# Loading the value windows of the first batch ahead of the weight stages, and weight stages through GpSimd's queue

## The chip, the cores and the metric

The kernel runs on one core of a Trainium2 chip. The metric is the time of one execution on the device in microseconds (us). A profile records one execution: its span runs from the first to the last instruction of the core.

## The reference

Four batches, eight heads, 576 positions, 64 values per head. Three stages follow one another:

```
# attention, per head, two parts that are added
out_d     = softmax(scale * mean4(q) @ mean4(k).T) @ mean4(v)       # 144 x 144, on means of 4 positions
out_local = softmax over |i - j| < 4 of (scale * q @ k.T)  @ v      # a band of 7 keys
x = repeat4(out_d) + out_local                                      # laid out as (batch, 576, 512)

# first gated layer
h = relu(x @ w_in)                        # 512 -> 1024
x = (h * sigmoid(conv3(h))) @ w_out       # 1024 -> 512

# second gated layer
out = (sigmoid(conv5(x)) * (x @ w_val)) @ w_out2
```

`w_in`, `w_out`, `w_val`, `w_out2` and the two convolutions' weights come as 64-bit floats; the kernel turns them into 32-bit floats itself, and splits each into a high and a low part for three matmuls in the place of one.

## The kernel before

**Work.** Attention goes by head pairs, four a batch, sixteen steps `s` in all. A step `s` has eight slots (`att_slots`, which stands in the big function): scores of the band (`loc_s`), scores of the means (`down_s`), then in slots 2 and 3 the values of the *step before* (`loc_av`, two halves) between the normalisations (`loc_n`, `down_n`), in slots 4 and 5 the transposes of the next head pair's k and q (`prep_k`, `prep_q`), and in slots 6 and 7 the rest. `prep_q` also averages v over four positions (`pool_v`: two adds on VectorE, tiles `ldv` and `vd`). The results of `loc_av` are tile `xo`.

**Two forms of v.** `pool_v` reads v in tile `ldv`. `loc_av` reads v by key blocks of 32 positions, in tile `ldw`: for each of 24 blocks of queries the 32 keys around it. For the first batch, `load_v_first` (L270) brings `ldv` in two halves (head pairs 0 and 1, then 2 and 3), and `load_vw_first` (L283) brings `ldw` for all eight heads in 24 loads of 64 KB. For later batches `load_v` (L239) and `load_vw` (L302) do it step by step.

**Weights.** `Weights` keeps a list of 16 jobs: eight pieces of `w_in`, then eight of `w_out`, each 128x512 (512 KB of 64-bit numbers). `load` issues the transfer of the next piece into one of three `stage` buffers (two for the last ones); `split` turns a landed piece into 32 bits (one step on ScalarE, tile `stage`, then four on VectorE) and into its parts (one on ScalarE, one on VectorE, tiles `win` and `wout`). Three loads stand ahead of the steps; each later load follows a split, and its transfer waits until the last reader of its buffer is done: eight at places listed in `EARLY`, the others between matmul units of the first batch.

**Order.** Every transfer is issued on SyncE's queue (SP). SP issues in order. The program gives SP's loads eight completion counters in turn, so that a load also waits until the load eight places before it has landed. The order on the other engines is set when the program is built, by a scheduler that estimates when each operand will be there; `ordered` pins it for the steps of the first batch (PE, VectorE, ScalarE), `beneath` lets the splits fill in between. ScalarE (ACT), VectorE (DVE) and SP run what they have strictly in that order. Nearly all instructions of DVE and ACT have line L151 and those of PE L141, which are the helpers that record them, so tiles are named instead.

Of the kernel before, what the change touches and what calls it, by code (L numbers as in the profile page):

```python
# [10 lines left out]
I32 = mybir.dt.int32  # L11
# [52 lines left out]
def kernel(  # L64
# [13 lines left out]
    nc = tc.nc  # L78
# [5 lines left out]
    HP = H // 2  # L84
# [15 lines left out]
    PW = 512  # L100
# [33 lines left out]
    def key_start(j):  # L134

        return min(max(QB * j - 4, 0), S - KB)
# [54 lines left out]
    class Weights:  # L191
# [10 lines left out]
            self.staged = []  # L202
            self.n = 0

        def load(self):
            if not self.jobs:
                return
            dst, src, j, f0 = self.jobs.pop(0)
            rows = src[j * 128 : j * 128 + 128]
            t, w = self.stage(self.n)  # L210
            self.n += 1
            if src.dtype == F32:
                nc.sync.dma_start(out=w, in_=rows[:, f0 : f0 + PW])
            else:
                nc.sync.dma_start(out=t, in_=rows.bitcast(I32)[:, 2 * f0 : 2 * (f0 + PW)])
            self.staged.append((t, w, src.dtype == F32, dst, j, f0))

        def split(self):
# [18 lines left out]
    def load_v(b, hp):  # L237
        t = ap.tile([HD, 2, 2, 4, D], F32, tag="ldv", name="ldv", bufs=1)
        nc.sync.dma_start(  # L239
            out=t.rearrange("p e s r d -> p e s (r d)"),  # L240
            in_=v[b, 2 * hp : 2 * hp + 2].rearrange("h (s p r) d -> p h s (r d)", s=2, r=4),
        )
        T["ldv", b, hp] = t
# [20 lines left out]
    def load_v_first(part):  # L264

        if part == 0:
            first["v"] = keep.tile([HD, H, 2, 4, D], F32, tag="wout1", name="ldv")
        n = H // 2
        t = first["v"][:, part * n : part * n + n]
        nc.sync.dma_start(  # L270
            out=t.rearrange("p h s r d -> p (h s) (r d)"),
            in_=v[0, part * n : part * n + n].rearrange("h (s p r) d -> p (h s) (r d)", s=2, r=4),
        )
        for hp in range(part * HP // 2, (part + 1) * HP // 2):
            T["ldv", 0, hp] = first["v"][:, 2 * hp : 2 * hp + 2]

    def load_vw_first():

        vw = keep.tile([128, NG, H, D], F32, tag="wout0", name="ldw")
        for g in range(NG):  # L280
            for c in range(4):
                k0 = key_start(c * NG + g)
                nc.sync.dma_start(  # L283
                    out=vw[KB * c : KB * c + KB, g], in_=v[0, :, k0 : k0 + KB].rearrange("h k d -> k h d")
                )
        for hp in range(HP):
            T["ldw", 0, hp] = vw[:, :, 2 * hp : 2 * hp + 2]
# [241 lines left out]
    def prep_k(s):  # L529
        transp(T.pop(("ldk", *where(s))), "k", scale)  # L530
        if HP <= s + 1 < NSTEP:
            load(k, "ldk", *where(s + 1))

    def prep_q(s):
        transp(T.pop(("ldq", *where(s))), "q", 1.0)
        pool_v(*where(s))
        if HP <= s + 1 < NSTEP:
            load(q, "ldq", *where(s + 1))
            load_v(*where(s + 1))
# [212 lines left out]
            unit(fn)  # L752

    make_identity(nc, ident)
    for hp in range(HP):
        load(k, "ldk", 0, hp)
        load(q, "ldq", 0, hp)
        if hp % 2 == 0:
            load_v_first(hp // 2)
    for h in HT:  # L760
        nc.gpsimd.memset(h, 0.0)
    nc.gpsimd.memset(mask, 0.0)
# [4 lines left out]
    for c, g, n, off in spans + [(0, 0, 1, 0), (3, NG - 1, 1, QB * (NB - 1) - key_start(NB - 1))]:  # L767
        m = m3[32 * c : 32 * c + 32, g : g + n]
        for sgn in (1, -1):
            nc.gpsimd.affine_select(  # L770
                out=m,
                in_=m,
# [11 lines left out]

    W = Weights([(win, w_in), (wout, w_out)], stage)

    nw = 3 * KF + 5 * KM
    cw = mp.tile([nw, 384], I32, tag="cv", name="cw", bufs=3)
    cwf = cw[:, 256:].bitcast(F32)
    for src, o, m in ((conv3, 0, 3 * KF), (conv5, 3 * KF, 5 * KM)):  # L790
        if src.dtype == F32:
            nc.sync.dma_start(out=cwf[o : o + m], in_=src.rearrange("t (f p) -> (t f) p", p=128))
        else:
            nc.sync.dma_start(
                out=cw[o : o + m, :256], in_=src.bitcast(I32).rearrange("t (f p) -> (t f) p", p=256)
# [6 lines left out]
        mm(p[:, :nw], cwf, ident[:nw, :nw], is_transpose=True)  # L802
        vec.tensor_copy(cwt, p[:, :nw])

    for _ in range(3):
        W.load()
    load_vw_first()
    load_v(1, 0)
    load(k, "ldk", 1, 0)
    load(q, "ldq", 1, 0)  # L810
# [122 lines left out]
```

## Time and profile before

| | |
|---|---|
| median of 3 runs | 521.6 us (517.53 to 523.5) |
| the profiled execution | 523.79 us |
| its span | 521.7 us |
| PE busy | 453.0 us (87%) |
| DVE busy | 358.2 us (69%) |
| ACT busy | 266.0 us (51%) |
| POOL (GpSimd) busy | 6.1 us (1%), 25 instructions |
| moved by DMA | 39.58 MB, mean 76 GB/s |
| mean granted TensorE clock | 0.905 |

PE's share is high over the span as a whole, but not in its first third: the page's slices of 13 us show PE at 4 to 7 tenths up to about 120 us, and at 9 for most of the time behind it. The row "PEclk" of the same slices gives the granted clock, which is at half (1.2 GHz of 2.4) from 26 us to some 90 us.

### The profile page before, as it was taken

How to read it: one execution, taken by the hardware profiler on the slowest of the kernel's cores; microseconds unless marked ns; L12 is line 12 of the kernel's file. 1: busy time of each engine (PE TensorE's matmuls, PEld its weight loads, DVE VectorE, ACT ScalarE, POOL GpSimd, SP SyncE). 2: the span in 40 equal slices, each digit the busy share in tenths (PEclk: the TensorE clock that was granted, in tenths of full speed). 3: DMA queues.
4: the chain of work that ended last, by engine and by line, in shares of the span. 5: the costliest groups of instructions: out<-in, count | busy, mean ns of one | idle time of the engine just before them, and what ended most of it. 6: DMA issues, size and time to landing. Idle time of an engine off the chain costs nothing.

```text
span 521.7 us, 13808 instructions
## 1 busy us (share of the span) xinstructions
PE 453.0 (87%) x5961; PEld 412.7 (79%) x5961; DVE 358.2 (69%) x655; ACT 266.0 (51%) x564; POOL 6.1 (1%) x25
## 2 busy tenths in 40 slices
PE   5747565468977999899899999999968999999997
PEld 4546544357976999899899889999958999889885
DVE  3517678789997344897866799503989999964130
ACT  1504535467784443877545678414877365542122
POOL 4000000000000000000000000000000000000000
PEclk9955556598998999999799999999987999999999
DMA  8957124343441214224133121003112000120102
GB/s 204 222 130 164 52 82 114 113 132 111 119 113 29 67 43 93 48 58 98 28 74 79 37 64 32 14 21 122 40 41 81 10 33 2 60 102 20 62 21 102
DMA packets 70963, 39.58 MB, mean 76 GB/s; under 512 B 59050, under 2 KB 65526, under 8 KB 70902
## 3 DMA queue, kind: packets, MB, share of 16 engines
q1 hardware_dynamic: 70902, 38.70, 28.0%
q8 instruction: 47, 0.77, 0.6%
q14 instruction: 14, 0.11, 0.1%
HBM read 33.96 MB, written 4.72 MB: 74 GB/s over the span
## 4 chain that ended last, share of the span: by engine, by line
PE 59%; DVE 21%; DMA 9%; ACT 7%; SPq 2%; issue 1%; ACTq 0%; DVEq 0%
PE pb L141 19%; PE pa L141 12%; PE pc L141 10%; PE pd L141 10%; DVE cv L151 5%; DVE stage L151 4%; PE avl L141 3%; DMA ldv<-in_v_dram 3%; DMA stage<-in_moe_w_in_dram 2%; ACT ed L151 2%; DMA ldq<-in_q_dram 2%; DVE hglo L151 2%; SPq L283 1%; PE tp L141 1%; DMA stage<-in_moe_w_out_dram 1%
## 5 line engine op out<-in xcount | busy, mean ns | idle before, releaser
L141 PE MATMUL pb<-hghi,wout 128*128 128x288 f32 x512 | 105.5, 314 | 4.7 <-ACT hghi L151 4.7
L141 PE MATMUL pa<-xhi,win 128*128 128x288 f32 x512 | 103.0, 308 | 3.6 <-DVE xo L151 3.6
L141 PEld LDWEIGHTS pb<-hghi,wout 128*128 128x128 f32 x512 | 80.6, 197 | 8.6 <-ACT hghi L151 5.6
L141 PEld LDWEIGHTS pa<-xhi,win 128*128 128x128 f32 x512 | 78.1, 192 | 6.9 <-DVE xo L151 3.9
L141 PE MATMUL pb<-hglo,wout 128*128 128x288 f32 x256 | 57.5, 307 | 2.0 <-DVE hglo L151 2.0
L151 DVE SCALAR_TENSOR_TENSOR cv<-h,cwt,cv 128x576 f32<-128x576 f32 x64 | 51.9, 811 | 7.5 <-ACT cv L151 7.1
L141 PE MATMUL pa<-xlo,win 128*128 128x288 f32 x256 | 55.5, 299 | 0.0
L141 PE MATMUL pc<-ys,wval 128*128 128x288 f32 x384 | 51.3, 294 | 0.0
L141 PEld LDWEIGHTS pc<-ys,wval 128*128 128x128 f32 x384 | 51.1, 188 | 0.3
L151 DVE SCALAR_TENSOR_TENSOR g<-y,cwt,g 128x576 f32<-128x576 f32 x64 | 49.5, 814 | 0.0
L141 PEld LDWEIGHTS avl<-et,ldw 32*64 32x64 f32 x1536 | 30.1, 150 | 22.3 <-issue 8.5
L141 PE MATMUL avl<-et,ldw 32*64 32x24 f32 x1536 | 34.2, 227 | 15.5 <-DMA ldw<-in_v_dram 9.2
L141 PEld LDWEIGHTS pb<-hglo,wout 128*128 128x128 f32 x256 | 43.0, 197 | 3.5 <-DVE hglo L151 3.4
L141 PE MATMUL pd<-wout,hghi 128*128 128x512 f32 x144 | 44.7, 394 | 0.0
L141 PEld LDWEIGHTS pa<-xlo,win 128*128 128x128 f32 x256 | 42.0, 193 | 0.0
L151 DVE TENSOR_TENSOR xo<-avl,od 128x288 f32<-128x288 f32 x32 | 14.2, 444 | 32.3 <-PE avl L141 32.3
L151 ACT ACTIVATE ed<-ed,smd 72x144 f32<-72x144 f32 x64 | 21.4, 404 | 23.6 <-DVE smd L151 23.6
L141 PEld LDWEIGHTS pd<-wout,hghi 128*128 128x128 f32 x144 | 26.7, 187 | 6.3
L151 ACT ACTIVATE cv<-cv 128x576 f32<-128x576 f32 x32 | 21.9, 683 | 15.3 <-DVE cv L151 14.9
L151 DVE TENSOR_TENSOR hglo<-cv,hghi 128x576 fp32r<-128x576 f32 x32 | 24.1, 753 | 6.8 <-ACT hghi L151 6.8
L151 ACT ACTIVATE hghi<-cv 128x576 fp32r<-128x576 f32 x32 | 21.8, 680 | 13.0 <-DVE cv L151 12.9
L151 ACT ACTIVATE ed<-sd,mxd 72x144 f32<-72x144 f32 x64 | 23.3, 370 | 10.0 <-DVE mxd L151 9.2
(87 smaller groups left out, 695.2 us busy)
## 6 DMA issues: line engine op xcount, KB each, us to landing
stage<-in_moe_w_out_dram SPq DMA_DIRECT2D x12, 512.0 KB
out_dram<-o SPq DMA_DIRECT2D x18, 256.0 KB
stage<-in_moe_w_in_dram SPq DMA_DIRECT2D x8, 512.0 KB
ldv<-in_v_dram SPq DMA_DIRECT2D x13, 288.0 KB
ldk<-in_k_dram SPq DMA_DIRECT2D x26, 144.0 KB
ldq<-in_q_dram SPq DMA_DIRECT2D x26, 144.0 KB
ldw<-in_v_dram SPq DMA_DIRECT2D x48, 48.0 KB
stage<-in_moe_w_val_dram SPq DMA_DIRECT2D x4, 512.0 KB
```

Of the source, the lines that this page charges most:

```text
L141: last["pe"] = nc.tensor.matmul(*a, **kw)
L151: last[self.key] = getattr(self.engine, name)(*a, **kw)
L283: nc.sync.dma_start(out=vw[KB * c : KB * c + KB, g], in_=v[0, :, k0 : k0 + KB].rearrange("h k d -> k h d"))
```

## The change

`Weights.load` gets an argument `queue` that is GpSimd's queue unless another is named; the first three loads name SP. So the five other pieces of `w_in` and the eight of `w_out` are issued by GpSimd (POOL), and only the first three by SP. At the start, only head pairs 0 and 1 of k and q and the first half of v are issued first; then come the 24 loads of `load_vw_first`, then the three weight stages, then k and q of head pairs 2 and 3 with the second half of v between them. Sizes, buffers and arithmetic are the same.

```diff
-        def load(self):
+        def load(self, queue=nc.gpsimd):
...
             if src.dtype == F32:
-                nc.sync.dma_start(out=w, in_=rows[:, f0 : f0 + PW])
+                queue.dma_start(out=w, in_=rows[:, f0 : f0 + PW])
             else:
-                nc.sync.dma_start(out=t, in_=rows.bitcast(I32)[:, 2 * f0 : 2 * (f0 + PW)])
+                queue.dma_start(out=t, in_=rows.bitcast(I32)[:, 2 * f0 : 2 * (f0 + PW)])
...
-    for hp in range(HP):
+    for hp in range(2):
         load(k, "ldk", 0, hp)
         load(q, "ldq", 0, hp)
-        if hp % 2 == 0:
-            load_v_first(hp // 2)
+        if hp == 0:
+            load_v_first(0)
+    load_vw_first()
...
     W = Weights([(win, w_in), (wout, w_out)], stage)
 
+    for _ in range(3):
+        W.load(nc.sync)
+    for hp in range(2, HP):
+        load(k, "ldk", 0, hp)
+        load(q, "ldq", 0, hp)
+        if hp == 2:
+            load_v_first(1)
...
-    for _ in range(3):
-        W.load()
-    load_vw_first()
     load_v(1, 0)
```

On SP, from its start, the program before has this order (72x8x256 is a half of v, 32x8x64 one load of the key blocks):

```order
L252 DMA ldk<-in_k_dram 96x2x384
L252 DMA ldq<-in_q_dram 96x2x384
L270 DMA ldv<-in_v_dram 72x8x256
L252 DMA ldk<-in_k_dram 96x2x384
L252 DMA ldq<-in_q_dram 96x2x384
L252 DMA ldk<-in_k_dram 96x2x384
L252 DMA ldq<-in_q_dram 96x2x384
L270 DMA ldv<-in_v_dram 72x8x256
L252 DMA ldk<-in_k_dram 96x2x384
L252 DMA ldq<-in_q_dram 96x2x384
L794 DMA cw<-in_moe_conv_w_dram 24x256
L794 DMA cw<-in_moe_conv_w_dram 20x256
L215 DMA stage<-in_moe_w_in_dram 128x1024 x3
L283 DMA ldw<-in_v_dram 32x8x64 x24
```

And with the change:

```order
L252 DMA ldk<-in_k_dram 96x2x384
L252 DMA ldq<-in_q_dram 96x2x384
L270 DMA ldv<-in_v_dram 72x8x256
L252 DMA ldk<-in_k_dram 96x2x384
L252 DMA ldq<-in_q_dram 96x2x384
L283 DMA ldw<-in_v_dram 32x8x64 x24
L215 DMA stage<-in_moe_w_in_dram 128x1024 x3
L252 DMA ldk<-in_k_dram 96x2x384
L252 DMA ldq<-in_q_dram 96x2x384
L270 DMA ldv<-in_v_dram 72x8x256
L252 DMA ldk<-in_k_dram 96x2x384
L252 DMA ldq<-in_q_dram 96x2x384
```

The key blocks moved ahead of the weight stages and of five loads that steps 2 and 3 read; the second half of v now stands behind all of these.

On ACT, in the first matmul units of the first batch, the order before and the order now differ from the place where the first piece of `w_out` is converted. One piece of it before (`h`, `cv`: gate of the first layer; `stage`: first conversion step of a weight piece; `od`: result of the means' attention):

```order
L151 ACTIVATE h_78<-pa 128x576
L151 ACTIVATE cv<-h_78,cwt 128x576
L151 ACTIVATE stage<-stage 128x512
L151 ACTIVATE od<-avd 128x144
L151 ACTIVATE wout_1223<-stage 128x512
L151 ACTIVATE cv<-cv 128x576
```

And now:

```order
L151 ACTIVATE h_78<-pa 128x576
L151 ACTIVATE cv<-h_78,cwt 128x576
L151 ACTIVATE od<-avd 128x144
L151 ACTIVATE wout_1223<-stage 128x512
L151 ACTIVATE stage<-stage 128x512
L151 ACTIVATE cv<-cv 128x576
```

The conversion of a piece, which waits for a transfer, stands behind `od` now. DVE's order changes in the same stretch in the same manner, some rows up and some down; PE's order is the same throughout.

## Rows read from the trace of the kernel before

**Rows 1.** Engines by stretch: from:to, length, busy us (instructions), clock, DMA share, GB/s.
```profile
0.00:20.00 20.00, 13.04 (x216) 11.53 (x218) 8.49 (x19) 7.59 (x19) 5.62 (x21) 1.00 0.93 215
20.00:40.00 20.00, 10.72 (x226) 8.57 (x224) 5.36 (x14) 2.36 (x10) 0.00 (x0) 0.67 0.66 156
...
40.00:60.00 20.00, 14.61 (x302) 12.65 (x300) 14.40 (x35) 9.05 (x25) 0.00 (x0) 0.50 0.46 108
140.00:160.00 20.00, 14.76 (x200) 13.42 (x202) 20.00 (x39) 15.59 (x33) 0.11 (x1) 0.99 0.30 77
...
180.00:200.00 20.00, 20.00 (x333) 18.68 (x332) 8.14 (x18) 7.82 (x21) 0.00 (x0) 1.00 0.28 67
```

**Rows 2.** Waits, whole span: engine and tile, waited for, total us, times, longest.
```profile
DVE xo L151 <- PE avl L141: 32.3, 7, 13.1
```

**Rows 3.** SP's queue in the first 40 us: start, length, line, tile, count.
```profile
10.12 1.32 SPq L794 DMA_DIRECT2D cw<-in_moe_conv_w_dram  x2
12.34 2.61 SPq L215 DMA_DIRECT2D stage<-in_moe_w_in_dram  x3
19.77 16.21 SPq L283 DMA_DIRECT2D ldw<-in_v_dram  x24
```

**Rows 4.** Chain that ended last, first 40 us: start, length, what.
```profile
14.62 11.93 DMA stage<-in_moe_w_in_dram
...
29.89 0.45 SPq L283
...
30.38 1.65 SPq L283
...
35.04 1.99 DMA ldw<-in_v_dram
```

**Rows 5.** Timeline 22 to 49 us: start, length, instruction, [idle before, releaser].
```profile
22.35 1.14 PE L141 MATMUL sd<-kd,qd 64*72 64x144 f32 x8
24.33 0.17 DVE L151 TENSOR_SCALAR mxd<-mxd 72x4 f32<-72x4 f32 x1
...
37.60 0.46 DVE L151 TENSOR_TENSOR xo<-avl,od 128x288 f32<-128x288 f32 x1 [13.11 <-PE avl L141]
...
43.60 0.68 DVE L151 TENSOR_TENSOR ldv<-ldv 72x512 f32<-72x512 f32 x1
...
48.14 0.63 ACT L151 ACTIVATE win<-stage 128x512 fp32r<-128x512 f32 x1 [1.81 <-DVE stage L151]
```

**Rows 6.** The same chain further on, transfers in it.
```profile
90.16 3.57 DMA stage<-in_moe_w_out_dram
...
108.54 4.28 DMA ldv<-in_v_dram
...
161.71 3.33 DMA ldv<-in_v_dram
```

**Rows 7.** Timeline 93 to 167 us, instructions behind a transfer.
```profile
93.81 0.66 ACT L151 ACTIVATE stage<-stage 128x512 f32<-128x512 f32 x1 [0.98 <-DMA stage<-in_moe_w_out_dram]
...
99.77 0.66 ACT L151 ACTIVATE stage<-stage 128x512 f32<-128x512 f32 x1 [3.35 <-DMA stage<-in_moe_w_out_dram]
...
111.81 0.66 ACT L151 ACTIVATE stage<-stage 128x512 f32<-128x512 f32 x1 [1.98 <-DMA stage<-in_moe_w_out_dram]
...
112.70 0.50 PE L141 MATMUL sl<-maskr,identr 128*128 128x256 f32 x2 [2.00 <-ACT od L151]
...
112.84 0.69 DVE L151 TENSOR_TENSOR ldv<-ldv 72x512 f32<-72x512 f32 x1 [1.41 <-DMA ldv<-in_v_dram]
...
166.54 0.54 PE L141 MATMUL pb<-hglo,wout 128*128 128x288 f32 x2 [0.43 <-DVE hglo L151]
```

**Rows 8.** POOL's timeline at the start, the twelve steps that build the mask.
```profile
2.55 4.39 POOL L770 TENSOR_SCALAR_AFFINE_SELECT mask<-mask 32x160 f32<-32x160 f32 x12
```

**Rows 9.** Instructions on tile `stage`: duration ns min/median/max, first and last start.
```profile
L151 DVE TENSOR_SCALAR stage<-stage x32: 375/418/429, 45.8 to 154.3; 128x512 f32<-128x512 f32 x16, 128x512 int32<-128x512 int32 x16
L151 DVE SCALAR_TENSOR_TENSOR stage<-stage x32: 643/682/694, 46.7 to 157.3; 128x512 int32<-128x512 int32 x32
```

## The prediction

> **What bounds the kernel now.** I read the engines by stretch first. In the first 20 us the DMA engines are taken for 0.93 of the time and move 215 GB/s: transfers set the pace. From 20 to 40 us nothing is full: PE 10.7 of 20 us, VectorE 5.4, ScalarE 2.4, DMA 0.66. From 140 to 160 us VectorE works all 20 us, and from 180 us on PE does [rows 1]. So three regimes follow one another: transfers, then the chain of small steps over VectorE, ScalarE and PE, then PE. The stretch of 20 to 40 us, where all are idle, is the one to ask about. The waits name it: VectorE waits longest for `xo` on PE, 32.3 us in total, and 13.1 us at one time [rows 2]. In the timeline that one time is step 1: PE ends `down_s` at 23.5 (22.35 + 1.14), VectorE its `mxd` at 24.5, and `xo`, which should come next, runs at 37.60 [rows 5]. SP's queue says why: the 24 loads of the key blocks start only at 19.77 and take 16.21 us to issue [rows 3], and the chain of waits runs through them until the last has landed at 37.03 (35.04 + 1.99) [rows 4].
>
> **The head, part one: the key blocks come earlier.** In the new order they are loads 6 to 29 of SP's queue. Each load waits for the landing of the one eight places before. Load 11, now and before, waits for the first half of v, and load 13 for the second q; before, these two were the first `cw`, issued at 10.12, and the first stage, issued at 12.34 [rows 3]. The loads ahead of them are unchanged, so the same landings release the 6th and the 8th key block. Sixteen remain, at 0.49 us each (0.45 and a gap of 0.04), with one of 1.65 in their like before [rows 4]: 12.34 + 16 x 0.49 = 20.2, or 21.4 with the long one. I take 21.0. The last lands 1.99 us later [rows 4], at 23.0, before PE is through `down_s`. So `xo` can run at about 24.9 in place of 37.60: 12.7 us earlier. This is the upper bound of what the head can give.
>
> **Part two: what is late next.** Behind the key blocks SP issues three stages, k and q of head pair 2, and the second half of v. The transposes of step 1 need k and q, and VectorE, in its order, stops at `ldv` (before: 43.60 [rows 5]) until the second half of v is there. First stage issued at 21.4; one that goes alone lands after 3.57 us [rows 6], at 25.0. For each further one I take 1.5 us: from 19.77, when the second half of v has landed and releases SP, to 26.57, when the third stage has (14.62 + 11.93), two loads of k and q and three stages pass [rows 3, 4]; k or q takes 1.14 (two landings between the stage issues at 12.34 and 14.62 [rows 3, 4]), so (6.8 - 2.3) / 3 = 1.5. Third stage 28.0, k 29.1, q 30.3. The half of v took 5.15 us behind q before (14.62 to 19.77 [rows 3, 4]): 35.4. VectorE then does at 35.4 what it did at 43.60: **8.2 us earlier**. The chain over k and q gives about the same: q lands at 30.3, its transposes and ScalarE's steps follow.
>
> The ends of this term: 12.7 us if the loads behind come in time; if the three stages need the 11.93 us that the third took in the crowded head [rows 4], instead of 3.57 + 3.0, v lands at 40.7 and 2.9 us are left. I take 8.2, since the DMA engines are at 0.66 in that stretch [rows 1], far from the 0.93 of the crowded one.
>
> The convolution weights now land behind all of this, at about 38. ScalarE converts them just ahead of `win`, for which it sat idle 1.81 us [rows 5]; that cover, shifted, reaches to 39.3. Cost nothing; if they come later, their lateness is the cost. The first batch-1 loads follow them; they are used from step 4 on, behind 90 us, and cost nothing.
>
> **Steps 2 and 3** have the same instructions in the same order on all engines, at the same half clock [rows 1], with k and q of head pair 3 landed at about 38 for a use near 54. The shift of 8.2 us is carried through.
>
> **The stages on GpSimd's queue.** SP's issue of a stage is some 0.35 us, and SP is not what waits; taking 13 of them away from SP gives nothing by itself. What SP's queue gains is that loads of k, q and v don't stand behind a stage that waits. At 108.54 the load of v was released by its own tile, not by the stage ahead of it, so this gain is about nothing too. On the other side stands d, by how much a stage from GpSimd lands later than one from SP. The trace of before has none. Below, d = 0; above, a whole second transfer, 3.6 us [rows 6]. I take 0.8, about two of GpSimd's own small steps of 0.37 (4.39 / 12) [rows 8]. For the pieces of `w_in` d is hidden: they land 7 to 15 us ahead of their split. Pieces of `w_out` are not: ScalarE stood 0.98, 3.35 and 1.98 us before three of them [rows 7].
>
> **The stretch from 90 to 166 us**, with its new order. The first piece costs d, since the conversion still stands ahead of the exponentials. The second, where 3.35 stood, now travels beside some 2 us of steps that were queued behind it; d and a step that moved behind it take 1.3 back: 0.7 gained. `od` goes ahead of the third piece, so PE's 2.00 us before `sl` go; but VectorE is the full engine there, and it meets the wait for v (1.41 [rows 7]) again, since v is still loaded only when the tile before is used up, and then a second one of about 1 us: its next load of v has two steps fewer ahead of it. At the sixth piece some five us lie between the release of its buffer and its own first step, about what a transfer and its conversion need; with d, 0.5 is lost. Last, `hglo` goes ahead of the wait for v at 161.71, so PE's 0.43 [rows 7] goes. Sum: -0.8 + 0.7 - 1.0 - 0.5 + 0.43, and up to 2.0 for `sl`: I call it nil, with 3 us to either side. Behind 166 us PE is full, nothing is changed, and the shift reaches the end.
>
> **Sum.** 523.8 (the profiled execution) - 8.2 = 515.6. The profiled execution lies 2.2 above the median of the three runs, so in terms of the median 521.6 - 8.2 = **513.4 us**.
>
> **Rivals.** One per cent, 5.2 us, is about what a measurement of this kernel tells from no change; I use it as the bound.
>
> *The loads behind the key blocks come too late.* The stages and v land as slowly as in the crowded head: 2.9 us are left, 518.7, within 1%. For it: the order puts 1.6 MB ahead of k and q. Against it: the idle DMA engines between 20 and 40 us. Chance 0.15.
>
> *The head is freed wholly*, because v needs less than 5.15 us on an emptier queue and the middle gains by `od`: 12.7 us, 508.9. Chance 0.12.
>
> *GpSimd can't issue in time where VectorE is full.* VectorE's TENSOR_SCALAR on 128x512 takes 0.42 us, SCALAR_TENSOR_TENSOR on as many elements 0.68 [rows 9]; if the quick form holds something that GpSimd needs, each stage waits for a gap, and VectorE has none in that stretch [rows 1]. Four pieces of `w_out` are exposed, two with nothing and two with about 2 us ahead of them, so the loss is 4d - 4. With d = 2.5, two thirds of the way from 0 to 3.6, it is 6.0 of the 8.2: 519.4, within 1%. Chance 0.12. The Trainium skill, page "SBUF — State Buffer", section "SBUF: two separate sides", states such a rule: while VectorE runs an operation that uses both of its ports, GpSimd can't write the descriptors of a transfer that it issues, and a transfer of 620 ns took 3100 ns beside such operations (section "A bandwidth-pool intuition that's wrong"). By that figure d would be an estimated 2.5 us for every load. No run here shows it yet.
>
> *Slower: the same, with d past 3.* At d = 3.05 the loss in the middle eats the head's gain; at d = 4.5 it is 14 us, 5.8 slower than before: 527.4. That needs a transfer from GpSimd to land after 8 us where SP's took 3.6. Nothing in this trace comes near. Chance 0.05.
>
> *The key blocks don't come earlier*, because 256 B pieces choke the crowded engines at the start: then `xo` stays near 37 and nothing is gained, 521.6. While such loads were issued, from 20 to 36 us, the engines stood at 0.66 [rows 1]: 0.02.
>
> **Numbers.** The forecast keeps 0.54. Its own range is 5.2 to 11 us of gain, 510.5 to 516.5. Faster by over 1%: 0.54, the 0.12 of the freed head and some of the edges, 0.69 in all. Within 1%: 0.26. Slower: 0.05. The range that leaves 2 in 10 out: from 508 (a little past the freed head) to 519.5 (the late loads and d = 2.5).
>
> **What would show it.** In the changed kernel's trace: the last key block lands at 23 and the first long `xo` wait is gone; VectorE's `ldv` of step 1 is the new wait, ending near 35.4, on the second half of v; the same two instants 43.60 and 90.16 of before come 8 us earlier; stages issued by GpSimd land within 4.5 us of the release of their buffer; PE full from about 158 us. Wrong would be an `ldv` that runs at 31 or at 40, ScalarE standing over 4 us before pieces of `w_out`, or steps 2 and 3 longer than before.

## The result

The changed kernel takes **514.8 us** (median of 4 runs, 511.9 to 516.2) beside 520.9 us for the kernel before on the same chip (4 runs, 517.5 to 523.5). The ratio is 0.987, with a 95% interval of 0.983 to 0.990: faster by 6.1 us. (All ratios leave disturbed runs out, so one can differ a little from the quotient of two medians.) The profiled execution took 515.7 us with a span of 513.9. Its lines come in the order in which the prediction read them.

The engines by stretch, changed kernel (from:to, length, busy us of PE, PEld, VectorE, ScalarE, GpSimd with instructions, granted clock, DMA share, GB/s):

```profile
0.00:20.00 20.00, 11.60 (x210) 9.89 (x210) 7.75 (x18) 7.54 (x19) 5.62 (x21) 0.91 0.71 152
20.00:40.00 20.00, 12.98 (x275) 10.95 (x275) 10.65 (x24) 6.72 (x20) 0.00 (x0) 0.50 0.87 217
```

Against [rows 1], VectorE works 10.7 us in place of 5.4 between 20 and 40 us: there the gain shows. But the transfers tell a second thing. In the first 20 us they fell from 215 to 152 GB/s, some 1.3 MB less, and from 20 to 40 they rose from 156 to 217. Bytes were put off, not saved.

The waits of `xo` over the whole span, changed kernel:

```profile
DVE xo L151 <- PE avl L141: 16.7, 7, 11.6
```

The timeline around step 1 (start, length, instruction, idle before and releaser), changed kernel:

```profile
25.90 0.46 DVE L151 TENSOR_TENSOR xo<-avl,od 128x288 f32<-128x288 f32 x1 [0.56 <-PE avl L141]
32.84 2.19 PE L141 MATMUL tp<-ident,ldk 96*64 96x96 f32 x24 [6.18 <-DMA ldk<-in_k_dram]
35.06 0.65 ACT L151 ACTIVATE kT<-tp 128x576 f32<-128x576 f32 x1 [4.54 <-PE tp L141]
37.16 0.69 DVE L151 TENSOR_TENSOR ldv<-ldv 72x512 f32<-72x512 f32 x1 [0.67 <-DMA ldv<-in_v_dram]
```

`xo` came 11.7 us earlier than in [rows 5], and where it waited 13.1 us [rows 2] it waits 0.56 (the longest wait left, 11.6, is at 340 us). What is late next is k of head pair 2: PE stood 6.18 us for it, ScalarE and VectorE behind PE. The second half of v held VectorE 0.67 us more. `ldv` ran 6.4 us earlier than before.

SP's queue, changed kernel, which answers [rows 3]:

```profile
3.11 18.17 SPq L283 DMA_DIRECT2D ldw<-in_v_dram  x24
21.32 2.54 SPq L215 DMA_DIRECT2D stage<-in_moe_w_in_dram  x3
23.91 0.43 SPq L252 DMA_DIRECT2D ldk<-in_k_dram  x1
24.39 1.08 SPq L252 DMA_DIRECT2D ldq<-in_q_dram  x1
25.51 0.69 SPq L270 DMA_DIRECT2D ldv<-in_v_dram  x1
...
31.66 0.31 SPq L239 DMA_DIRECT2D ldv<-in_v_dram  x1
```

The chain that ended last shows the first of the three stages by itself (start, length, what), and SP's own waits from 20 to 45 us show when the third had landed (total us, times, longest):

```profile
21.32 1.59 SPq L215
```

```profile
SPq L239 <- DMA stage<-in_moe_w_in_dram: 2.3, 1, 2.3
```

The load at 31.66, eight places behind the third stage, had to wait for that stage to land. So the three stages were issued from 21.32 and all there at 31.6. The engines by stretch again, in pieces of 2 us:

```profile
16.00:18.00 2.00, 1.75 (x29) 1.42 (x26) 0.82 (x3) 1.50 (x7) 0.00 (x0) 0.85 0.59 132
22.00:24.00 2.00, 2.00 (x105) 1.81 (x104) 0.76 (x2) 0.00 (x0) 0.00 (x0) 0.50 0.27 67
30.00:32.00 2.00, 0.00 (x0) 0.00 (x0) 0.76 (x1) 0.52 (x1) 0.00 (x0) 0.50 1.07 259
```

While SP issues key blocks of 64 KB, one in 0.49 us, the DMA engines are at 0.59 and move 132 GB/s. From 22 to 24 us they are at 0.27. Then three stages, k, q, v and the rest travel together, at 0.85 and 0.89 from 24 to 28 us and at 0.99 to 1.10 behind it. k was issued at 23.91 and used at 32.84.

GpSimd's issues of stages, three of thirteen, in the timeline of the changed kernel:

```profile
84.02 0.53 POOL L215 DMA_DIRECT2D stage<-in_moe_w_out_dram  x1 [10.73 <-DVE win L151]
90.11 0.62 POOL L215 DMA_DIRECT2D stage<-in_moe_w_out_dram  x1 [5.57 <-DVE win L151]
122.60 0.53 POOL L215 DMA_DIRECT2D stage<-in_moe_w_out_dram  x1 [0.74 <-DVE wout L151]
```

The chain that ended last, same stretch (start, length, what):

```profile
90.11 4.07 DMA stage<-in_moe_w_out_dram
122.60 6.88 DMA stage<-in_moe_w_out_dram
```

And ScalarE's first conversion steps of these pieces, the first, the second and the seventh of `w_out`:

```profile
87.74 0.66 ACT L151 ACTIVATE stage<-stage 128x512 f32<-128x512 f32 x1 [1.32 <-DMA stage<-in_moe_w_out_dram]
94.27 0.68 ACT L151 ACTIVATE stage<-stage 128x512 f32<-128x512 f32 x1 [1.49 <-DMA stage<-in_moe_w_out_dram]
129.50 0.67 ACT L151 ACTIVATE stage<-stage 128x512 f32<-128x512 f32 x1 [1.49 <-DMA stage<-in_moe_w_out_dram]
```

From the issue to the first conversion step it is 3.72 and 4.16 us for the first two; from SP it was 3.65 (90.16 to 93.81 [rows 6, 7]). The first two are not the whole story. Over all thirteen stages from GpSimd, a landing took 3.6 to 6.9 us from the issue, 4.1 in the median, and 4.2 in the median of the eight pieces of `w_out`, beside 3.57 for the one from SP [rows 6]. Three of the eight took 4.9 us or more: the fourth (100.94 to 106.06), and the sixth and seventh, which were issued at 121.33 and 122.60, travel together and were used at 126.23 and 129.50.

How the shift travels is read from one instruction that every step has, `mxl` on VectorE. Its starts in the profiles, in us, with the steps counted from 0 as in `s`, so that step 4 is head pair 0 of the second batch. The last two columns have two profiles each, which the experiments explain:

| step | before | change | order only | k, q, v and `cw` first, GpSimd | the same, all on SP |
|---|---|---|---|---|---|
| 2 | 49.6 | 43.2 | 44.2 | 37.6 / 36.7 | 37.9 / 38.4 |
| 4 | 90.0 | 83.6 | 84.6 | 78.0 / 77.1 | 79.0 / 80.5 |
| 5 | 115.8 | 107.2 | 111.2 | 101.6 / 100.9 | 104.8 / 106.6 |
| 6 | 139.0 | 133.7 | 134.6 | 126.7 / 126.2 | 129.8 / 131.2 |
| 7 | 166.4 | 160.6 | 162.0 | 153.4 / 153.1 | 157.3 / 158.6 |
| 11 | 248.6 | 241.5 | 243.6 | 233.8 / 234.8 | 238.5 / 240.2 |
| 12 | 268.8 | 259.3 | 261.4 | 251.6 / 252.6 | 256.3 / 260.5 |
| 15 | 328.6 | 319.5 | 321.4 | 311.6 / 312.6 | 316.3 / 320.5 |

The change's shift is 6.4 us up to step 4, 8.6 at step 5, 5.3 at step 6, 5.8 at step 7, and 7.1 at step 11. Between steps 11 and 12 it grows by 2.4, and there the two profiles differ in the clock. Kernel before, then changed kernel, by stretch:

```profile
250.00:260.00 10.00, 9.56 (x133) 9.21 (x134) 7.84 (x18) 6.54 (x18) 0.00 (x0) 0.66 0.12 28
```

```profile
241.00:251.00 10.00, 8.50 (x148) 8.00 (x147) 7.72 (x18) 5.16 (x17) 0.00 (x0) 1.00 0.07 17
```

The stretch of before ran partly at the lower of the two levels (1.2 of 2.4 GHz). The changed kernel does the same work nine microseconds earlier and has no such fall. That execution of before took 523.8 us, 2.2 over the median of its runs, and of the other profiles here only three have a fall between 170 and 370 us. So these 2.4 of the 7.8 us between the two spans are best put down to the one execution and not to the change.

The other way, some is lost again further on. The same stretch of work, kernel before and then changed kernel:

```profile
387.00:407.00 20.00, 15.30 (x88) 13.96 (x88) 20.00 (x34) 13.04 (x22) 0.00 (x0) 0.74 0.18 54
```

```profile
378.00:398.00 20.00, 15.96 (x80) 14.57 (x81) 20.00 (x34) 12.88 (x21) 0.00 (x0) 0.66 0.17 53
```

Both have a fall of the clock here, and the change's is longer (0.66 against 0.74). The shift goes from 9.2 to 8.3 us across it, and to 7.8 at the end. That the clock is the reason is likely, but not shown.

### The profile page after: what moved, and what is told of

Same layout as the page of the kernel before. It is cut to its first block, busy times and chain, and to the rows that moved or that the text cites. A ratio compares the mean times of both kernels' runs of the same rounds, so it can differ in the third digit from the quotient of the medians.

```text
span 513.9 us, 13813 instructions
## 1 busy us (share of the span) xinstructions
PE 451.5 (88%) x5961; PEld 412.6 (80%) x5961; DVE 358.5 (70%) x655; ACT 265.8 (52%) x564; POOL 13.3 (3%) x38
## 4 chain that ended last, share of the span: by engine, by line
PE 47%; DVE 20%; DMA 12%; issue 10%; ACT 7%; SPq 3%; POOL 1%; ACTq 0%; POOLq 0%; DVEq 0%
PE pb L141 14%; PE pc L141 10%; PE pd L141 10%; PE pa L141 9%; DVE cv L151 6%; DMA ldv<-in_v_dram 5%; DMA ldk<-in_k_dram 4%; DVE hglo L151 2%; ACT ed L151 2%; DMA stage<-in_moe_w_out_dram 2%; DVE g L151 2%; SPq L283 2%; PE avl L141 2%; DVE stage L151 1%; DVE mxd L151 1%
## 5 line engine op out<-in xcount | busy, mean ns | idle before, releaser
L141 PE MATMUL pb<-hghi,wout 128*128 128x288 f32 x512 | 103.7, 310 | 4.1 <-ACT hghi L151 4.1
L141 PE MATMUL pa<-xhi,win 128*128 128x288 f32 x512 | 106.0, 315 | 1.3 <-DVE xo L151 1.3
L141 PEld LDWEIGHTS pb<-hghi,wout 128*128 128x128 f32 x512 | 79.2, 194 | 8.0 <-ACT hghi L151 5.0
L141 PEld LDWEIGHTS pa<-xhi,win 128*128 128x128 f32 x512 | 81.0, 199 | 4.7 <-issue 2.3
L141 PE MATMUL pa<-xlo,win 128*128 128x288 f32 x256 | 56.9, 305 | 0.0
L141 PEld LDWEIGHTS pa<-xlo,win 128*128 128x128 f32 x256 | 43.2, 198 | 0.0
L141 PEld LDWEIGHTS avl<-et,ldw 32*64 32x64 f32 x1536 | 29.1, 158 | 15.7 <-issue 6.8
L141 PE MATMUL avl<-et,ldw 32*64 32x24 f32 x1536 | 32.1, 233 | 9.5 <-DVE xo L151 4.4
L151 ACT ACTIVATE cv<-cv 128x576 f32<-128x576 f32 x32 | 21.8, 681 | 15.7 <-DVE cv L151 15.6
L141 PE MATMUL tp<-ident,ldk 96*64 96x96 f32 (+1 forms) x168 | 18.2, 331 | 12.5 <-DMA ldk<-in_k_dram 10.3
L141 PE MATMUL pd<-wout,hglo 128*128 128x512 f32 x72 | 28.0, 395 | 0.0
```

The lines of the kernel that those rows point to most:

```text
L141: last["pe"] = nc.tensor.matmul(*a, **kw)
L151: last[self.key] = getattr(self.engine, name)(*a, **kw)
```

## The experiments

Each time is a median beside runs of the kernel before on the same chip; the ratio is to those. The diffs are against the changed kernel, but for two that say so.

One thing goes with the queue and has to be known for all that follows. No edit here moves a queue alone. With the stages on SP, the scheduler puts the steps of ScalarE and VectorE in the order of the kernel before; with the stages behind the first three on GpSimd, in the order of the change. The traces show it: the order alone, and the better order with all stages on SP, run exactly the steps of before in their order; the queue alone, k, q and v first, the better order with GpSimd, and the split behind the masks run exactly those of the change. All stages on GpSimd, the two versions with loads between the masks, and two buffers for v have orders of their own. So "the queue" below is the queue and the order of steps that comes with it.

### The order of loads alone

```diff
-        def load(self, queue=nc.gpsimd):
+        def load(self, queue=nc.sync):
```

> The new order of loads alone: every stage is issued by SP, as before the change. Theory (the gain comes from the key blocks' earlier place on SP's queue, and GpSimd's queue gives nothing): 513 to 516 us, within 2 us of the change; `xo` runs at 25.5 to 26.5, VectorE's `ldv` at 36.5 to 37.5 as in the change, since both queues are alike up to the fourth stage. Rival (GpSimd's queue carries part of the gain, because loads of k, q and v then stand behind SP's waiting stages): 517 to 520 us, with `ldv` waits behind 90 us that are 2 us or more longer than the change's.

**515.7 us, ratio 0.989 (0.982 to 0.995).** `xo` ran at 25.57, as expected, `ldv` at 38.18, a little later than expected. The order of loads brings the gain, with the steps in their old order too; a difference of 0.9 us to the change lies within the intervals. In the table, `mxl` of step 5 is 4.0 us behind the change's and that of step 6 only 0.9. Queue and order of steps together win some 3 us in the one step and lose nearly as much in the next. Which of the two does what is not shown.

### The queue alone

```diff
-    for hp in range(2):
+    for hp in range(HP):
         load(k, "ldk", 0, hp)
         load(q, "ldq", 0, hp)
-        if hp == 0:
-            load_v_first(0)
-    load_vw_first()
+        if hp % 2 == 0:
+            load_v_first(hp // 2)
...
+    for _ in range(3):
+        W.load(nc.sync)
+    load_vw_first()
     load_v(1, 0)
```

> The old order of loads, with all stages after the first three on GpSimd's queue. Theory (the queue is worth nothing and a stage from GpSimd lands 0.3 to 0.8 us later than one from SP): 519.5 to 523 us, within 1.5 us of the kernel before; `xo` at 37.6, `ldv` at 43.6; a w_out stage's split starts 4.0 to 4.4 us after its buffer is released, where SP's took 3.7. Rival one (GpSimd can't issue beside a full VectorE, d = 2.5 or more): 526 us or more, splits 6 us or more after the release. Rival two (the queue carries part of the gain): 519 us or less, the time gained between 90 and 166 us.

**520.4 us, ratio 0.997 (0.994 to 1.001).** The theory holds: queue and new order of steps together are worth nothing that can be measured. GpSimd's issues of stages beside a VectorE that works nearly all the time, here:

```profile
90.41 0.53 POOL L215 DMA_DIRECT2D stage<-in_moe_w_out_dram  x1 [10.73 <-DVE win L151]
96.48 0.62 POOL L215 DMA_DIRECT2D stage<-in_moe_w_out_dram  x1 [5.54 <-DVE win L151]
```

```profile
94.10 0.66 ACT L151 ACTIVATE stage<-stage 128x512 f32<-128x512 f32 x1 [1.29 <-DMA stage<-in_moe_w_out_dram]
100.36 0.68 ACT L151 ACTIVATE stage<-stage 128x512 f32<-128x512 f32 x1 [1.22 <-DMA stage<-in_moe_w_out_dram]
```

These two took 3.7 and 3.9 us from issue to use, a little less than the expected 4.0 to 4.4. Over all thirteen, landings took 3.6 to 6.9 us, 4.0 in the median; none reached the 8 us of the slower rival. (The first of these fences is GpSimd's timeline, the second ScalarE's.)

### k, q and v ahead of the stages

```diff
+    load(k, "ldk", 0, 2)
+    load(q, "ldq", 0, 2)
+    load_v_first(1)
     for _ in range(3):
         W.load(nc.sync)
-    for hp in range(2, HP):
-        load(k, "ldk", 0, hp)
-        load(q, "ldq", 0, hp)
-        if hp == 2:
-            load_v_first(1)
+    load(k, "ldk", 0, 3)
+    load(q, "ldq", 0, 3)
```

> The change, with k, q of head pair 2 and the second half of v issued by SP before the three first stages and not behind them. Theory (the head's gain stopped at 6.4 us because k, q and v stand behind three stages): k lands near 28 in place of 32.8, `ldv` runs at 31 to 33.5 in place of 37.2, 3 to 5 us more are gained, 510 to 512 us. Rival one (the DMA engines' total sets the time of `ldv`, whatever the order): `ldv` still at 36 or later, 514 to 516 us. Rival two (the stages now come late and ScalarE's `cw`, `win` work waits for them and holds up the exponentials of step 2): `ldv` near 32, but the exponentials of the next step no earlier than in the change, 514 us or more.

**512.8 us, ratio 0.983 (0.977 to 0.989).** This is 2.0 us better than the change and just misses the expected 510 to 512. VectorE's `ldv` and `mxl`, then ScalarE's `cw`, in the timeline:

```profile
30.77 0.68 DVE L151 TENSOR_TENSOR ldv<-ldv 72x512 f32<-72x512 f32 x1
39.67 0.54 DVE L151 TENSOR_REDUCE mxl<-sl 128x12 f32<-128x384 f32 x1
```

```profile
37.80 0.31 ACT L151 ACTIVATE cw<-cw 44x128 f32<-44x128 f32 x1 [3.44 <-DMA cw<-in_moe_conv_w_dram]
```

The three stages did hold `ldv`: without them it runs 6.4 us earlier still, with no wait. Of these, 3.5 us reach `mxl` (43.2 to 39.7). The rest is the second rival with another name in it: not the stages, but the convolution weights, last in the queue, hold ScalarE 3.44 us, and it stands ahead of the exponentials.

### The first stages on GpSimd's queue too

```diff
     for _ in range(3):
-        W.load(nc.sync)
+        W.load()
```

> The change, with the three first stages on GpSimd's queue too, which issues them in the first microseconds, beside SP's first loads. Theory (the DMA engines stand at 0.6 while SP issues small key blocks one at a time; three stages from another queue fill that gap, and k, q, v no longer stand behind them): `ldv` at 29 to 33, 510 to 513 us. Rival (the stages take their share of the DMA engines from the first v, k, q, which are what step 0 waits for, and from the key blocks, whose issue waits for landings eight places before): the first transposes and `xo` come 2 to 4 us later, `ldv` gains at most 1 to 2 us, 514 to 518 us.

**515.5 us, ratio 0.987 (0.981 to 0.993).** The rival. The last key block was issued at 27.2 in place of 21.3, and VectorE:

```profile
29.02 0.46 DVE L151 TENSOR_TENSOR xo<-avl,od 128x288 f32<-128x288 f32 x1 [6.25 <-PE avl L141]
35.98 0.69 DVE L151 TENSOR_TENSOR ldv<-ldv 72x512 f32<-72x512 f32 x1 [0.88 <-DMA ldv<-in_v_dram]
```

`xo` lost 3.1 us, `ldv` gained 1.2. The first 20 us moved 205 GB/s again, but with stages that nobody needs yet.

### The convolution weights ahead of the stages too

```diff
     load_v_first(1)
-    for _ in range(3):
-        W.load(nc.sync)
-    load(k, "ldk", 0, 3)
-    load(q, "ldq", 0, 3)
     nw = 3 * KF + 5 * KM
...
+    for _ in range(3):
+        W.load(nc.sync)
+    load(k, "ldk", 0, 3)
+    load(q, "ldq", 0, 3)
```

> k, q and the second half of v ahead of the three first stages, as in the experiment before, and the two loads of the convolution weights ahead of these stages too; no instruction of another engine moves. There ScalarE stood 3.44 us before `cw` (37.80), and VectorE's `mxl` came at 39.67, 9.9 us earlier than in the kernel before, though `ldv` came 12.8 earlier. Theory (the last thing late in the head is `cw`): `cw` at 34.4 or earlier, no wait before it, `mxl` at 36.5 to 38, 2 to 3 us more than with k, q, v first alone, 509.5 to 511.5 us. Rival (DMA engines are at their total from 24 to 40 us, so that the stages take over the wait): ScalarE's wait before its first `stage` grows from 1.07 to 3 us or more, `mxl` at 39 or later, 512 to 514 us.

**508.3 us, ratio 0.976 (0.972 to 0.981).** VectorE and ScalarE in the timeline:

```profile
31.56 0.69 DVE L151 TENSOR_TENSOR ldv<-ldv 72x512 f32<-72x512 f32 x1 [0.69 <-DMA ldv<-in_v_dram]
32.83 0.67 ACT L151 ACTIVATE stage<-stage 128x512 f32<-128x512 f32 x1 [2.35 <-DMA stage<-in_moe_w_in_dram]
35.54 0.31 ACT L151 ACTIVATE cw<-cw 44x128 f32<-44x128 f32 x1
```

The wait for `cw`, 3.44 us, is gone; 1.28 us of it come back before the first stage (2.35 in place of 1.07), so `cw` runs at 35.54 and not by 34.4 as the theory said. `mxl` runs at 37.6, 2.1 us earlier than with k, q, v alone, and the time is better than the 509.5 that was expected at best. The head is now 12.0 us ahead of the kernel before. That is most of the 12.7 that the prediction gave as the upper bound. From 24 to 40 us the DMA engines stand at 1.02, and the two waits that are left in these lines are for transfers.

### Half of the key blocks from GpSimd, between its masks

```diff
-    def load_vw_first():
+    def load_vw_first(part):
...
+        queue = (nc.sync, nc.gpsimd)[part]
-        for g in range(NG):
+        for g in range(part * NG // 2, (part + 1) * NG // 2):
...
-                nc.sync.dma_start(
+                queue.dma_start(
```

The first half stays in its place, the second stands behind the code of the masks. This version has the order of k, q and v first; the next one has the convolution weights first as well.

> k, q and the second half of v ahead of the three first stages, and 12 of the 24 key blocks issued by GpSimd, between its masks, while SP issues the other 12. Theory (what holds the head's transfers back is SP, which issues one key block of 64 KB in 0.49 us, and not the DMA engines): DMA share from 12 to 20 us 0.8 or more in place of 0.57, the last key block issued by 16, k of head pair 2 issued by SP at 16 to 18 in place of 22.4 and landed by 23; `xo` stays at 24 to 26, since the steps before it set it; `cw` is then no longer late, and the time is 508 to 512 us if VectorE's and ScalarE's changed order costs nothing. Rival (small packets are slow in the engines themselves): DMA share stays at 0.6, k issued at 20 or later, nothing gained over the one queue. Second rival (GpSimd's masks come late behind its loads): the first `sl` and `xo` 2 us or more later, 514 us or more.

**521.2 us, ratio 0.998 (0.995 to 1.002).** The second rival, and much of it: GpSimd ran seven loads ahead of its masks and five in their midst, and the first step waited for the masks (the waits, whole span):

```profile
DVE maskr L151 <- POOL mask L774: 14.5, 1, 14.5
```

The theory's own signs were there too. SP issued k of head pair 2 at 16.59, and from 14 to 16 us the DMA share was 1.25. So it is SP's issue, not the engines, that left them at 0.59.

### Both edits

> Both of the edits before: the convolution weights ahead of the stages, and half of the key blocks on GpSimd's queue. Theory (the head is a sum of late transfers, and each edit takes one away): the head ends at its chain of steps, `mxl` at 36 to 37.5, 508 to 511 us, 1 us or less ahead of the better of the two. Rival (with `cw` early there is nothing left that the second queue could win): as the convolution weights first alone, within 1 us.

**520.0 us, ratio 1.000 (0.997 to 1.003).** Neither the theory nor its rival: the late masks, again with `sl` of the first step some 9 us late, hide everything else. The version told nothing beyond the one before.

### Two buffers for batch 1's v

```diff
-        t = ap.tile([HD, 2, 2, 4, D], F32, tag="ldv", name="ldv", bufs=1)
+        t = ap.tile([HD, 2, 2, 4, D], F32, tag="ldv", name="ldv", bufs=2)
...
-        vd = ap.tile([HD, 2, 2, D], F32, tag="vd", name="vd")
+        vd = ap.tile([HD, 2, 2, D], F32, tag="vd", name="vd", bufs=1)
```

> The change, with two buffers for batch 1's v in place of one (and one for its reduced form `vd` in place of two, for the room). Theory (VectorE's waits for v, 15.7 us in ten places, lie partly on the path behind 150 us, since v is loaded only when the tile before is used up): the waits for `ldv` behind 60 us fall under 2 us in sum, and 3 to 6 us are gained, 509 to 512 us. Rival (PE is full there, and takes the waits up): the waits go, and the time stays within 1.5 us of the change, 513 to 516 us.

**515.1 us, ratio 0.988 (0.984 to 0.992).** The time is the rival's, but its reason is not shown, because the waits did not go: `ldv` still waits 13.6 us in nine places (15.7 in ten in the change). SP's queue of this kernel from 167 us:

```profile
166.99 6.04 SPq L302 DMA_DIRECT2D ldw<-in_v_dram  x12
...
176.15 0.31 SPq L239 DMA_DIRECT2D ldv<-in_v_dram  x1
```

v stands behind 16 other loads of its step, and a second buffer does not move it. What these waits cost stays open.

### Half of the key blocks from GpSimd, behind its masks

The diff is against the version with both edits.

```diff
+    half = NG // 2
+    nc.gpsimd.tensor_copy(first["vw"][:, half:, 0, 0:1], mask[:, 0:half].rearrange("p (g o) -> p g o", o=1))
     load_vw_first(1)
```

> As with both edits (convolution weights early, 12 of the 24 key blocks issued by GpSimd), but GpSimd issues them behind its masks: one small copy of a few elements of the mask into the tile of the key blocks, which the loads then overwrite, keeps them there. Theory (the 14.5 us that VectorE waited for the mask were all that the two-queue version lost, and SP's issue of the key blocks is what holds k, q and v back): the first `sl` back at 8 to 9, SP issues k of head pair 2 at 13 to 18 in place of 21.0, VectorE's `ldv` runs at 30.5 without a wait, ScalarE's wait of 2.35 before its first stage goes, `mxl` 1 to 3 us earlier, 505.5 to 508 us. Rival (the DMA engines are the bound as soon as two queues feed them, and the landings that SP's loads wait for come later): the key blocks are all there at 20 as before, k issued at 18 or later, steps 0 and 1 no earlier or up to 4 us later, 508 to 512 us.

**510.7 us (505.4 to 514.0), ratio 0.975 (0.968 to 0.982).** Its interval contains that of the one queue, so the time decides nothing. The profile has signs of both. By stretch, then PE:

```profile
10.00:12.00 2.00, 0.36 (x4) 0.36 (x6) 1.97 (x4) 0.00 (x0) 2.00 (x5) 0.82 1.33 184
14.00:16.00 2.00, 2.00 (x30) 2.00 (x28) 1.66 (x6) 1.52 (x8) 1.40 (x3) 0.50 1.18 175
```

```profile
27.59 1.75 PE L141 MATMUL avl<-et,ldw 32*64 32x24 f32 x72 [3.55 <-issue]
```

For the theory: SP issued k at 15.46, `ldv` had no wait, and ScalarE's wait before its first stage was gone. For the rival: the DMA engines were full at 175 to 187 GB/s from 10 to 16 us, `ldv` ran at 34.57 and `mxl` at 40.6, each 3 us behind the one queue, and `xo` at 28.57. What PE stood for before its values, 3.55 us, the profile doesn't name. The key blocks themselves are not it by their landings: GpSimd issued the last of its twelve at 16.3, and the slowest landed 6.8 us after its issue, so all were there by about 23.1. Why the head became longer stays open.

### The better order with all stages on SP

The diff is against the version with the convolution weights first.

```diff
-        def load(self, queue=nc.gpsimd):
+        def load(self, queue=nc.sync):
```

> The best order so far (k, q, second half of v and the convolution weights ahead of the three first stages) with every stage issued by SP; up to the fourth stage nothing differs, so the head is the same (`ldv` at 30.8 to 31.6). Theory (GpSimd's queue is worth nothing, whichever head stands before it): 507 to 510 us, within 1.5 us of the same order with GpSimd's queue. Rival (with the head shorter, SP's queue becomes the late one, and loads of k, q, v behind waiting stages cost): 511 us or more, longer waits for `ldv` between 90 and 160 us.

**513.0 us, ratio 0.984 (0.981 to 0.988).** The time is the rival's: 4.7 us behind the same order with GpSimd's queue. One loss belongs to the queue, since it lies ahead of the place where the orders of steps part. On SP the fourth piece of `w_in` stands behind loads for batch 1 and is issued at 49.06; GpSimd issued it at 37.77. ScalarE then waits for it:

```profile
53.71 0.66 ACT L151 ACTIVATE stage<-stage 128x512 f32<-128x512 f32 x1 [2.43 <-DMA stage<-in_moe_w_in_dram]
```

With GpSimd's queue this wait isn't there. It is worth 0.6 us at `mxl` of step 3. Further on, two stages wait on SP's queue for their buffers, and ScalarE stands before a piece of `w_out`. Four lines, in this order: SP and ScalarE in this version, SP in the kernel before, ScalarE in the better order with GpSimd's queue:

```profile
79.06 6.14 SPq L215 DMA_DIRECT2D stage<-in_moe_w_out_dram  x2
```

```profile
88.47 0.66 ACT L151 ACTIVATE stage<-stage 128x512 f32<-128x512 f32 x1 [3.21 <-DMA stage<-in_moe_w_out_dram]
```

```profile
90.16 6.20 SPq L215 DMA_DIRECT2D stage<-in_moe_w_out_dram  x2
```

```profile
88.73 0.68 ACT L151 ACTIVATE stage<-stage 128x512 f32<-128x512 f32 x1 [1.38 <-DMA stage<-in_moe_w_out_dram]
```

It is tempting to put the 4.7 us down to the 6.14 us on SP's queue and the 3.21 us on ScalarE. The lines don't bear it out. The kernel before has the same wait on SP, and there the queue was worth nothing. And the piece is converted at 88.47 here and at 88.73 with GpSimd's queue, no later: ScalarE stands longer for it because with GpSimd's queue another step (`wout`, 86.72) stands ahead of the conversion, and here it doesn't; and VectorE's `xo`, which stands ahead of the split with GpSimd's queue (87.02), stands behind its first step here (89.50).

Since the time spoke against the first two experiments, both versions ran again, side by side, with no edit:

> The best order (k, q, second half of v and convolution weights ahead of the first stages; further stages on GpSimd's queue) once more, beside the same order with all stages on SP, both on one chip. Theory (the 4.7 us between the two medians are GpSimd's queue: on SP two stages that wait for their buffers hold the loads of k, q and v behind them, 6.14 us at 79.06, and a split waits 3.21 us at 88.47): 507 to 510 us, 3 us or more below the other. Rival (chips and single executions make the difference: a fall of the granted clock to 0.66 for 5 to 10 us, as at 150 us in the one profile and not in the other): the two medians within 1.5 us.

> The same order with every stage on SP's queue, once more, on the same chip as the one with GpSimd's queue. Theory (the queue is worth 3 us or more in this order): 511.5 to 514 us, and in the trace again `mxl` of head pair 0 in the next batch (101.6 with GpSimd's queue) 2.5 us or more later. Rival (chip and single executions): 508 to 511 us, within 1.5 us of the other.

**509.1 us, ratio 0.978 (0.975 to 0.981), and 511.9 us, ratio 0.984 (0.981 to 0.986).** These intervals overlap by a hair, those of the first pair just miss each other: GpSimd's queue, with its order of steps, is worth about 3 us in this order of loads (2.8 here, 4.7 in the first pair, which ran on two chips). The expected 3 us or more were just missed by the one, and 511.9 was met by the other. `mxl` of step 5 came 5.7 us later, of which 1.7 stand already at step 2, and another 1.7 come with the late fourth piece of `w_in` by step 3. (The expectation calls the 101.6 head pair 0 of the next batch; it is head pair 1.)

Where the rest comes from, `mxl` shows in part (the table, and 90.0, 113.3 and 140.2 at steps 4 to 6 with the queue alone). There are four pairs of SP and GpSimd: before and the queue alone, the order alone and the change, and the two pairs in the better order. From step 4 to step 5 the version with GpSimd's queue is shorter by 2.3 to 3.0 us in all four. From step 5 to step 6 it is longer, by 3.6 and 3.0 us in the first two pairs, and by 0.2 and 0.7 us in the better order. So the better order keeps what the older ones give back. Waits for v go the same way: from 90 to 160 us `ldv` waits 3.1 and 2.8 us with SP, 0.8 and 1.0 with GpSimd. Why the better order keeps it, and what of it is the queue and what the order of steps, no run here shows.

## Why the prediction was right, and which size was off

**The key blocks come earlier: right.** Forecast were the last issue at 21.0 and `xo` at 24.9; measured, 21.3 and 25.9. With the order alone `xo` stayed at 25.57, with the queue alone it went back to 37.58. Step 0 had already run 0.9 us later (`mxl` at 12.8 in place of 11.9); with the queue alone, where the first loads are as before, it stands at 12.3, so part of this is the spread of single executions.

**What is late next: the right place, a wrong size.** The term that was too small is "3.57 + 3.0", the 6.6 us from the issue of the first stage to the landing of the third. It measured 10.3 us (21.32 to 31.6), close to the 11.93 that the prediction gave as the other end. The first stage was to land at 25.0 and landed at 27.2, the second followed after 1.6 us as forecast, the third after 2.8 in place of 1.5. k was to land at 29.1 and landed at 32.8. From k to the half of v it then took 4.4 us and not 6.3, which gave 1.9 us back: v was to land at 35.4 and landed at 37.1, and the 8.2 us became 6.4. Two errors of the sum partly cancelled.

I had taken 0.66 as the DMA share between 20 and 40 us [rows 1], as if the engines had room. But the same change made the 20 us before slow (132 GB/s while key blocks are issued), and the 1.3 MB that were not moved there had to be moved here. From 28 us on the engines were full, which fits the late third stage. It doesn't explain the first: the long issue that the prediction had budgeted among the key blocks fell on this stage (1.59 us), and from 22 to 24 us the engines were at 0.27. Why it took 5.8 us stays open. That the stages are what v stood behind is shown: taking them out of the way gave 3.5 us at `mxl`, `cw` another 2.1.

**Steps 2 and 3 carry the shift: right**, 6.4 at three `mxl` in a row (steps 2, 3 and 4).

**The queue gives nothing and d is 0.8: about right for this change.** The eight pieces of `w_out` landed 4.2 us after GpSimd's issue in the median, against 3.57 for the one from SP in [rows 6], so d is 0.6 in the median. But three of the eight lie beyond the 4.5 us that the prediction named, at 4.9 to 6.9. The Trainium skill, page "SBUF — State Buffer", section "SBUF: two separate sides", has the rule by which GpSimd can't write descriptors beside a two-port operation of VectorE, and its subsection "A bandwidth-pool intuition that's wrong (but worth ruling out)" a transfer of 620 ns that took 3100 ns. Here no issue of a stage took over 0.67 us, while VectorE was taken for 27.4 of the 30 us from 90 to 120. An effect of that size on every load this case does not show; a smaller one, or one on the three late landings, it can't exclude. That nothing is gained by taking the stages from SP does not hold for the better order, at least not for queue and order of steps together.

**The middle is nil within 3: right**, at -0.6 (6.4 to 5.8 at step 7). Its parts are less so. The sixth piece cost 0.53, as forecast; the first 0.3 rather than 0.8 (1.32 in place of 0.98); and the seventh, which the sum doesn't have, stood 1.49 us behind a landing of 6.88.

**The end: right by its median, by luck in the profile.** 513.4 was forecast, 514.8 measured; the 6.1 us gained are close to 6.4 in the head less 0.6 in the middle, though the interval, 5 to 9 us, would have let in other sums. The two spans differ by 7.8, close to 8.2, for reasons that the prediction didn't have: the shift grew from 5.8 to 7.1 between steps 7 and 11, for a reason that stays open, by 2.4 beside before's fall of the clock, and lost 0.9 beside the change's longer one near 390 us.

The rival with "the head is freed wholly" described what a better order reaches: 508.3 and 509.1, where it said 508.9.

## What to carry to other kernels

When a load is moved forward in a queue, ask what the queue moves per microsecond while it issues it: bytes that small loads keep from moving come back as a full DMA stretch, and the next wait stands there. Order the loads by first use down to the smallest (here two loads of 24 and 20 rows of convolution weights cost 2.1 us by being last). Judge a second queue again after the first is in order: with the order of steps that goes with it, it was worth nothing measurable before, and about 3 us after. And where a scheduler orders the steps, compare the order of every engine before you call an edit a change of one thing.

## What was not expected of the hardware

One queue that issues 64 KB loads of 256 B pieces kept the DMA engines at 0.57 to 0.61 and 130 to 139 GB/s; with two queues, behind the masks, they were full (1.18 to 1.33 from 10 to 16 us), but at only 175 to 187 GB/s, where larger pieces in the change got 231 to 346 at 0.99 to 1.10. So a full share is not a fixed rate.

The granted clock of a stretch need not be what its matmuls ran at. With the queue alone changed the profile gives 1.00 from 40 to 60 us, where the kernel before has 0.50 [rows 1]. But the transposes take 2.19 us in both, as elsewhere at 0.50, and 1.21 where k, q and v came first and the clock was at 1.00. Queue alone, by stretch and in the timeline, then k, q, v first, timeline:

```profile
40.00:60.00 20.00, 14.61 (x302) 12.65 (x298) 14.37 (x35) 9.06 (x25) 1.20 (x2) 1.00 0.47 107
```

```profile
53.31 2.19 PE L141 MATMUL tp<-ident,ldk 96*64 96x96 f32 x24
```

```profile
25.90 1.21 PE L141 MATMUL tp<-ident,ldk 96*64 96x96 f32 x24 [0.70 <-DVE sml L151]
```

And a fall of the clock where PE is full is worth as much as a small change. The shift grew by 2.4 us across the one of before. The repeat with all stages on SP has 0.71 from 240 to 250 us in its profiled execution, which took 515.6 where the median of its six is 511.9. Four of the fourteen profiles here have such a fall between 170 and 370 us, three of them between 244 and 259 and one at 290, so one profile of each kernel cannot tell a gain of 2 us.
